# Talking-heads attention and two gated dense stages on one core: the attention output taken through DRAM, with an even pace of dense work behind it

## Chip, core and metric

The kernel runs on one core of a Trainium2 chip. The metric is the device time of one execution in microseconds; the median of several runs is given. One execution is also profiled, and its time is a little different from the median.

## What is computed

The input is a batch of 4 with 12 heads of 448 positions and 64 elements. The scores of all heads are mixed across heads, put through a softmax, mixed across heads again and applied to `v`. The result, 1792 tokens of 768, goes through two dense stages.

```python
scores = scale * np.matmul(q, k.transpose(0, 1, 3, 2))
scores = np.einsum('bhij,hg->bgij', scores, w_pre)
attn = softmax(scores)                       # over the last axis
attn = np.einsum('bhij,hg->bgij', attn, w_post)
x = np.matmul(attn, v)                       # -> [1792, 768]
h = (x @ w1) * (x @ w2) @ w3                 # 768 -> 1024 -> 1024
x = h @ w_out                                # -> 768
h = np.maximum(np.maximum(x @ m1, x @ m2), x @ m3)
out = h @ m_out                              # 768 -> 768
```

## The kernel before

**Precision.** Most matmuls take operands split in two fp32r parts, `hi` (a cast) and `lo` (the rest), and make three products for each pair, in `products`, line 110, where it yields after every two pairs: one such piece of six matmuls is a unit of dense work. The weights come as 64-bit floats. `from_f64` turns a slab of 128 x 768 into fp32: a load of 768 KB into `wraw` (three buffers) on SP's queue, one ScalarE operation (line 91) and four VectorE operations (lines 92 to 95) into `wc` (three buffers). `slab` then makes `whi` on ScalarE and `wlo` on GpSimd for batch 0 or VectorE later (lines 155, 156; three buffers each). A slab once converted is stored to a DRAM tensor (`kept_a`, `kept_b`, `kept_m`, `kept_o`), and later batches load it from there, 384 KB.

**Attention.** `load_heads` loads the heads of batch 0, k on SP's queue and q on ScalarE's, into the buffers that later hold `X`. `scores` computes 112 rows of two heads and stores them to `sdram`; `regroup` loads them back by groups of ten rows and all heads. One step takes two groups: `split_scores` and `mix_softmax` (pre-mix, maximum, exponential, normalised post-mix matrix), and one step later `post_mix`. There are 23 steps a batch. After steps 5, 11, 17 and 22 `attend` multiplies the collected columns (120, the last time 88) with `v` and writes `X[b]`, that is `xhi` by ScalarE and `xlo` by VectorE, straight from PSUM. The scores of the next batch are computed in between.

**Dense work.** `fuse` multiplies `w3` and `w_out` of the first stage into one matrix `w34` (69 pieces), beside the attention of batch 0. `moe(b)` runs the dense layers of batch b as a generator: slabs `a` and `b` on `X`, then `w34`, then `m0` to `m2`, then `o`. It fetches two slabs ahead. `fill(rate / 3)`, called three times a step, takes as many pieces from the generators in line as the rate says; a surplus of credit stays. `moe(b)` joins the line when the attention of batch b has ended, so dense work of batch b runs beside the attention of batch b + 1, and that of batch 3 alone. `X` has one buffer. So a later batch may write it only when the layers that read it are through, and line 489 runs them to that point first if need be:

```python
since = s - LAG - (s - LAG) // NP * NP
rate = 3.4 if s < NP + LAG else (9.2 if since < CP - 1 else 6.2)
```

**Conversions ahead and stores.** During the attention of batch 0 eleven slabs (`before`, the first of the queue) are converted and stored ahead of use, one every second step. A store is issued in `wc` two conversions later, or, once `before` is empty, at the end of each step. The program text is turned into one instruction list per engine by a scheduler, so that the order on a queue can differ from that of the text.

Of the kernel before, what the change touches and what calls it, by code (L numbers as in the profile page):

```python
# [7 lines left out]
F32 = mybir.dt.float32  # L8
F32R = mybir.dt.float32r
# [6 lines left out]
B, H, S, D = 4, 12, 448, 64  # L16
NT, DM, DFF = B * S, 768, 1024
P = 128
# [5 lines left out]
KX, KH = DM // P, DFF // P  # L24
FW = DM // 2
PW = DM
LAG = 1
AHEAD = 2
NP = -(-NG // 2)
CP = CG // 2  # L30
# [11 lines left out]
def chunk(p):  # L42
    c = p // CP
    i0 = c * CG * GI
    return c, i0, min(CG * GI, S - i0)
# [3 lines left out]
def attention_talking_heads_moe_kernel(  # L49
# [16 lines left out]
    nc = tc.nc  # L66
    ps = ctx.enter_context(tc.tile_pool(name="ps", bufs=2, space=bass.MemoryType.PSUM))
    dram = ctx.enter_context(tc.tile_pool(name="dram", bufs=1, space=bass.MemoryType.DRAM))
    const = ctx.enter_context(tc.tile_pool(name="const", bufs=1))
    big = ctx.enter_context(tc.tile_pool(name="big", bufs=1))  # L70
    wp = ctx.enter_context(tc.tile_pool(name="wp", bufs=3))
    pa = ctx.enter_context(tc.tile_pool(name="pa", bufs=2))
    tmp = ctx.enter_context(tc.tile_pool(name="tmp", bufs=3))

    sdram = [dram.tile([S, H, S], F32, name=f"sdram_{b}") for b in range(B)]
    w34 = [dram.tile([KX // 2, P, KH * P], F32, name=f"kept_w34_{n}") for n in range(2)]
    kept = {("w34", m): w34[m // 3][m % 3] for m in range(KX)}

# [3 lines left out]
    def banks(tag):  # L82
        return ps.tile([P, 2, 512], F32, tag=tag, name=tag, bufs=1)
# [15 lines left out]
    def wc():  # L99
        turn["wc"] += 1  # L100
        while stores and stores[0][0] <= turn["wc"] - 2:
            nc.sync.dma_start(*stores.pop(0)[1:])
        return wp.tile([P, PW], F32, tag="wc", name="wc", bufs=3)

    def products(out, pairs, n_k):

        k = 0
        for x, (w_hi, w_lo, r_hi, r_lo) in enumerate(pairs):
            for w, r in ((w_hi, r_hi), (w_hi, r_lo), (w_lo, r_hi)):
                nc.tensor.matmul(out, w, r, start=(k == 0), stop=(k == 3 * n_k - 1))  # L110
                k += 1
            if x % 2:
                yield

# [8 lines left out]
    stored, stores = set(), []  # L125

    def convert(key):
        t = wc()
        from_f64(t, source[key], PW)
        stored.add(key)  # L130
        stores.append((turn["wc"], kept[key], t))
        return t
# [51 lines left out]
    def load_heads():  # L184

        t = [big.tile([P, HP, S], F32, tag=x, name=n) for x, n in (("xhi", "kall"), ("xlo", "qall"))]
        for a, z in ((0, 1), (1, 3), (3, HP)):
            for dst, src, eng in zip(t, (kT, qT), (nc.sync, nc.scalar)):
                eng.dma_start(dst[:, a:z], src[0, a:z].rearrange("x p j -> p x j"))
        return [[x[:, pr] for x in t] for pr in range(HP)]  # L190

    def load_pair(b, pr):
# [42 lines left out]
    def mix_softmax(b, p):  # L235
# [12 lines left out]
        nmax = pa.tile([120, 2], F32, tag="nmax", name="nmax", bufs=3)  # L248
        nc.vector.tensor_reduce(out=nmax[:r, :n], in_=pt[:r, :n, :S], axis=AX.X, op=ALU.max, negate=True)  # L249
        e = pa.tile([120, 2, S], F32, tag="e", name="e", bufs=LAG + 1)  # L250
# [37 lines left out]
    def load_v(b):  # L288
        t = pa.tile([JP, JC, H * D], F32, tag="v", name="v", bufs=1)
        nc.sync.dma_start(t, v[b].rearrange("(c p) e -> p c e", p=JP))  # L290
        vst[b] = t

    X = {}

    def attend(b, p):
        _, i0, n = chunk(p)
        a = ast.pop(b)
        if i0 == 0:
            X[b] = [big.tile([P, KX, S], F32R, tag=x, name=x) for x in ("xhi", "xlo")]
        pt = banks("s")[:, :, :3 * n].rearrange("p b (x i) -> p b x i", x=3)  # L300
        for pr in range(HP):
            for jc in range(JC):
                for o in range(2):
                    h = 2 * pr + o
                    nc.tensor.matmul(  # L305
                        pt[o * D:(o + 1) * D, pr // 3, pr % 3, :], vst[b][:, jc, h * D:(h + 1) * D], a[:, jc, h, :],
                        start=(jc == 0), stop=(jc == JC - 1),
                    )
        hi, lo = [t[:, :, i0:i0 + n].rearrange("p (b x) i -> p b x i", b=2) for t in X[b]]
        for x in range(2):  # L310
            nc.scalar.copy(hi[:, x], pt[:, x])
            nc.vector.tensor_sub(lo[:, x], pt[:, x], hi[:, x].bitcast(F32))

# [40 lines left out]
    def dense(wt, nk, xh, xl):  # L356
        hi, lo = wt
        pt = bank()
        yield from products(pt[:, :S], [(hi[:, k], lo[:, k], xh[:, k], xl[:, k]) for k in range(nk)], nk)
        return pt[:, :S]  # L360

    def scratch(name):
        return tmp.tile([P, S], F32, tag="t", name=name)

    ready, queue = [], []
    for b in range(B):
        queue += [(KX, (x, m), b) for m in range(KH) for x in "ab"]
# [4 lines left out]
    def weights():  # L372
        while queue and len(ready) < 2:
            fetch()
        return ready.pop(0)
# [4 lines left out]
            ready.append(slab(nk, key, nc.gpsimd if b == 0 else nc.vector))  # L380

    def moe(b):
        x = X[b]
        h = [big.tile([P, KH, S], F32R, tag=t, name=t) for t in ("hhi", "hlo")]
        for m in range(KH):
            pt = yield from dense(weights(), KX, *x)
            fetch()
            a = scratch("a_sb")
            nc.scalar.copy(a, pt)
            pt = yield from dense(weights(), KX, *x)  # L390
            fetch()
            nc.vector.tensor_mul(a, pt, a)  # L392
            nc.scalar.copy(h[0][:, m], a)
            nc.vector.tensor_sub(h[1][:, m], a, h[0][:, m].bitcast(F32))
        done.add(b)
        y = [big.tile([P, KX, S], F32R, tag=t, name=t) for t in ("yhi", "ylo")]
        for m in range(KX):
            pt = yield from dense(weights(), KH, *h)
            fetch()
            nc.scalar.copy(y[0][:, m], pt)  # L400
            nc.vector.tensor_sub(y[1][:, m], pt, y[0][:, m].bitcast(F32))
        z = [big.tile([P, KX, S], F32R, tag=t, name=t) for t in ("hhi", "hlo")]
        for m in range(KX):
            t = scratch("z32")
            for x in range(3):
                pt = yield from dense(weights(), KX, *y)
                fetch()
                if x == 0:
                    nc.scalar.copy(t, pt)
                else:  # L410
                    nc.vector.tensor_max(t, pt, t)  # L411
            nc.scalar.copy(z[0][:, m], t)
            nc.vector.tensor_sub(z[1][:, m], t, z[0][:, m].bitcast(F32))
        for m in range(KX):
            pt = yield from dense(weights(), KX, *z)
            fetch()
            o = scratch("o")
            nc.scalar.copy(o, pt)
            nc.scalar.dma_start(outT[m * P:(m + 1) * P, b * S:(b + 1) * S], o)

    done = set()

# [8 lines left out]
    for pr in range(HP):  # L433
        scores(0, pr, 0, first[pr], "mps"[pr % 3], nc.vector if pr % 2 else nc.scalar, row[:, 2 * pr:2 * pr + 2])
        if pr % 2:
            sl = slice(2 * pr - 2, 2 * pr + 2)
            nc.sync.dma_start(sdram[0][:JP, sl], row[:, sl])
    load_v(0)
    next(side)

    steps = [(b, p) for b in range(B) for p in range(NP)]
    for s in range(AHEAD):
        regroup(*steps[s])
    early = [(pr, it) for it in range(1, IT) for pr in range(HP)]
    before = [key for nk, key, b in queue[:11]]
    heads = {}

    def ahead_scores(b, p, third):
# [16 lines left out]
    def fill(n):  # L465
        nonlocal credit
        credit += n
        while credit >= 1 and fillers:
            credit -= 1
            if next(fillers[0], StopIteration) is StopIteration:  # L470
                fillers.pop(0)

    for s in range(len(steps) + LAG):
        if s < len(steps):
            if s + AHEAD < len(steps):
                regroup(*steps[s + AHEAD])
            if s + 1 < len(steps):
                split_scores(*steps[s + 1])
            mix_softmax(*steps[s])
        since = s - LAG - (s - LAG) // NP * NP  # L480
        rate = 3.4 if s < NP + LAG else (9.2 if since < CP - 1 else 6.2)
        for third in range(3):
            if s < len(steps):
                ahead_scores(*steps[s], third)
            if third == 2 and s >= LAG:
                b, p = steps[s - LAG]
                post_mix(b, p)
                if p == NP - 1 or p % CP == CP - 1:
                    while b > 0 and b - 1 not in done:
                        fill(1)  # L490
                    attend(b, p)
                    if p == NP - 1:
                        if b + 1 < B:
                            load_v(b + 1)
                        fillers.append(moe(b))
            fill(rate / 3)
        if not before:
            while stores:
                nc.sync.dma_start(*stores.pop(0)[1:])
        if s % 2 == 0 and before and s < NP:  # L500
            convert(before.pop(0))
    while fillers:
        fill(1)

# [43 lines left out]
```

## Time and profile before

| | us |
|---|---|
| median of 3 runs | 1369.45 (1368.67 to 1369.77) |
| time of the profiled execution | 1374.67 |
| its span, first to last instruction | 1372.8 |
| TensorE (PE) busy | 1268.9 |
| VectorE (DVE) busy | 734.5 |
| ScalarE (ACT) busy | 619.7 |
| GpSimd (POOL) busy | 291.7 |
| mean granted TensorE clock | 0.966 of full |

In a profile, PE is matmuls and PEld the loading of their stationary operand, which overlaps with them. SP is the engine that issues most transfers; a queue is called by its engine with a q behind it. An instruction that waits holds back all that is behind it on its engine. Line numbers (L110) are those of the kernel. A name as `wlo<-kept_m` is the tile written and what it is made from. In the chain of waits each piece has its start, its length and what it was. Idle time of an engine stands with what released it.

### The profile page before, as it was taken

The page shows a single profiled execution, that of the slowest core. Times are in us where ns is not written, and L with a number is a line of the kernel's source. Part 1 is how long each engine was busy: PE and PEld are TensorE (multiplying, and loading weights), DVE is VectorE, ACT ScalarE, POOL GpSimd, SP SyncE. Part 2 cuts the span into 40 slices and gives each one's busy share as a digit, 9 for nine tenths or more (in the row PEclk, how much of TensorE's full clock was granted, in tenths as well). Part 3 has the DMA queues.
Part 4 walks back from the last instruction along what each step waited for, and adds up shares of the span by engine and source line. Part 5 has one row for each costly group of instructions (what it writes and reads, how often), then busy time and mean ns, then how long its engine had stood idle before and what let it go on. Part 6 is the DMA issues. An engine that isn't in the chain of part 4 may idle for free.

```text
span 1372.8 us, 19674 instructions
## 1 busy us (share of the span) xinstructions
PE 1268.9 (92%) x7695; PEld 1068.6 (78%) x7695; DVE 734.5 (54%) x1020; ACT 619.7 (45%) x1138; POOL 291.7 (21%) x154
## 2 busy tenths in 40 slices
PE   4688798999999879899999999999999998899998
PEld 1346477778778768778888888789999997799998
DVE  2886555224835768734554555454555656344342
ACT  1454554455555545653443544543443434333332
POOL 0441100125353434521111112220121213000000
PEclk7889899999999989999999999999999999999999
DMA  9889798653655767544453545643432434033233
GB/s 269 254 260 319 211 296 299 202 173 118 196 192 163 232 227 237 191 153 123 134 163 110 163 144 164 183 126 113 123 118 91 131 105 139 17 110 121 94 114 110
DMA packets 90805, 229.51 MB, mean 167 GB/s; under 512 B 8468, under 2 KB 45352, under 8 KB 90712
## 3 DMA queue, kind: packets, MB, share of 16 engines
q1 hardware_dynamic: 69960, 186.89, 43.7%
q10 hardware_dynamic: 20656, 41.34, 9.2%
q8 instruction: 61, 1.00, 0.3%
q0 software_dynamic: 96, 0.02, 0.1%
q14 instruction: 32, 0.26, 0.1%
HBM read 165.30 MB, written 62.91 MB: 166 GB/s over the span
## 4 chain that ended last, share of the span: by engine, by line
PE 71%; DVE 10%; DMA 9%; ACT 5%; issue 3%; POOL 2%; SPq 0%; ACTq 0%; POOLq 0%
PE w L110 48%; PE p L276 8%; PE s L305 5%; PE m L110 4%; PE s L204 4%; DVE wc L94 2%; ACT e L253 2%; DVE wc L95 2%; DMA wraw<-in_w3T 2%; DMA wraw<-in_wa 2%; POOL wlo L156 1%; DMA wraw<-in_w_out 1%; PE m L242 1%; DVE nmax L249 1%; DMA qall<-in_qT 1%
## 5 line engine op out<-in xcount | busy, mean ns | idle before, releaser
L232 POOL TENSOR_TENSOR x<-x,xh 120x896 fp32r<-120x896 f32 (+1 forms) x69 | 151.9, 2201 | 556.2 <-DVE xh L231 445.3
L155 ACT CAST whi<-wlo 128x768 fp32r<-128x768 f32 (+1 forms) x155 | 134.6, 869 | 261.9 <-DMA wlo<-kept_m 68.9
L156 DVE TENSOR_TENSOR wlo<-wlo,whi 128x768 fp32r<-128x768 f32 (+1 forms) x138 | 147.6, 1069 | 162.1 <-ACT whi L155 161.8
L276 PEld LDWEIGHTS p<-kwr,e 120*112 120x112 f32 (+1 forms) x1440 | 165.6, 183 | 40.0 <-issue 25.1
L110 PE MATMUL w<-yhi,whi 128*128 128x448 f32 (+1 forms) x496 | 188.5, 380 | 5.1 <-DVE z L411 2.6
L110 PE MATMUL w<-ylo,whi 128*128 128x448 f32 (+1 forms) x496 | 182.5, 368 | 3.5 <-POOL ylo L324 2.9
L276 PE MATMUL p<-kwr,e 120*112 120x120 f32 (+1 forms) x1440 | 174.5, 275 | 10.1 <-DVE kwr L260 6.3
L110 PE MATMUL w<-yhi,wlo 128*128 128x448 f32 (+1 forms) x496 | 181.5, 366 | 0.0
L110 PE MATMUL w<-hhi,whi 128*128 128x448 f32 (+1 forms) x400 | 153.1, 383 | 5.3 <-DVE z L411 2.6
L253 ACT ACTIVATE e<-m,nmax 120x448 f32<-120x448 f32 x180 | 112.5, 630 | 98.4 <-DVE nmax L249 98.4
L110 PE MATMUL w<-hlo,whi 128*128 128x448 f32 (+1 forms) x400 | 146.6, 366 | 8.1 <-POOL hlo L324 6.5
L249 DVE TENSOR_REDUCE nmax<-m 120x2 f32<-120x896 f32 (+1 forms) x92 | 98.1, 1066 | 100.0 <-PE m L110 57.5
L110 PE MATMUL w<-hhi,wlo 128*128 128x448 f32 (+1 forms) x400 | 146.4, 366 | 1.7 <-POOL wlo L156 1.4
L110 PE MATMUL w<-xhi,whi 128*128 128x448 f32 x384 | 141.3, 370 | 3.6 <-DVE a_sb L392 3.1
L110 PE MATMUL w<-xlo,whi 128*128 128x448 f32 x384 | 140.6, 366 | 0.0
L110 PE MATMUL w<-xhi,wlo 128*128 128x448 f32 x384 | 140.6, 366 | 0.0
L283 ACT COPY a<-p 112x480 f32<-112x480 f32 (+1 forms) x184 | 92.1, 552 | 64.5 <-PE p L276 56.5
L110 PEld LDWEIGHTS w<-yhi,whi 128*128 128x128 f32 x496 | 94.4, 190 | 25.8 <-issue 13.1
L110 PEld LDWEIGHTS w<-ylo,whi 128*128 128x128 f32 x496 | 94.6, 191 | 15.1 <-POOL ylo L324 4.0
L110 PEld LDWEIGHTS w<-yhi,wlo 128*128 128x128 f32 x496 | 94.4, 190 | 7.7 <-issue 0.8
L257 DVE TENSOR_SCALAR den<-den 120x2 f32<-120x2 f32 (+1 forms) x92 | 67.9, 738 | 60.1 <-ACT e L253 60.0
L110 PEld LDWEIGHTS w<-hhi,whi 128*128 128x128 f32 x400 | 76.1, 190 | 30.4 <-issue 12.7
(78 smaller groups left out, 1881.6 us busy)
## 6 DMA issues: line engine op xcount, KB each, us to landing
x<-sdram SPq DMA_DIRECT2D x88, 420.0 KB, 4.4
sdram<-s ACTq DMA_DIRECT2D x78, 392.0 KB, 3.9
wlo<-kept_m SPq DMA_DIRECT2D x54, 384.0 KB, 3.0
wraw<-in_wm SPq DMA_DIRECT2D x18, 768.0 KB, 6.2
wlo<-kept_w SPq DMA_DIRECT2D x24, 512.0 KB, 3.5
wlo<-kept_a SPq DMA_DIRECT2D x30, 384.0 KB, 3.1
wlo<-kept_b SPq DMA_DIRECT2D x29, 384.0 KB, 3.0
wraw<-in_w3T SPq DMA_DIRECT2D x16, 512.0 KB, 6.7
```

The costliest lines, as they stand in the source:

```text
L94: nc.vector.scalar_tensor_tensor(ti, low, 29, ti, op0=ALU.logical_shift_right, op1=ALU.bitwise_or)
L110: nc.tensor.matmul(out, w, r, start=(k == 0), stop=(k == 3 * n_k - 1))
L155: nc.scalar.copy(hi, t)
L156: lo_eng.tensor_sub(lo, t, hi.bitcast(F32))
L204: nc.tensor.matmul(pt[:JP, o, :S], q[sl, it * JP:(it + 1) * JP], k[sl], start=True, stop=True)
L232: nc.gpsimd.tensor_sub(x[:r, :n], x[:r, :n].bitcast(F32), xh[:r, :n].bitcast(F32))
L249: nc.vector.tensor_reduce(out=nmax[:r, :n], in_=pt[:r, :n, :S], axis=AX.X, op=ALU.max, negate=True)
L253: nc.scalar.activation(e[:r, u], pt[:r, u, :S], AF.Exp, bias=nmax[:r, u:u + 1], scale=1.0, accum_out=den[:r, u:u + 1])
L257: nc.vector.tensor_scalar_add(den[:r, :n], den[:r, :n], 1e-9)
L276: nc.tensor.matmul(pt[:, jc // 2, jc % 2, :, u * GI:u * GI + m], e[:r, u, jc * JP:(jc + 1) * JP], kwr[:r, u].rearrange("p (g i) -> p g i", ...
L283: nc.scalar.copy(ast[b][:, 2 * x:2 * x + 2, :, off:off + w].rearrange("p c g i -> p (c g) i"), pt[:, x, :, :, :w].rearrange("p c g i -> p ...
L305: nc.tensor.matmul(pt[o * D:(o + 1) * D, pr // 3, pr % 3, :], vst[b][:, jc, h * D:(h + 1) * D], a[:, jc, h, :], start=(jc == 0), stop=(jc ...
```

## The change

- `attend` copies its PSUM result with ScalarE into a scratch tile and stores it to a DRAM tensor `xdram[b]` on ScalarE's queue. `load_x(b)` loads all of `X[b]` from there on SP's queue in two halves, and makes `hi` on ScalarE and `lo` on VectorE. It is called at three places in `moe(b - 1)` and at the start of `moe(b)`; it does nothing until the attention of batch b is complete.
- The guard on the layers that still read `X` is gone, and the rate is one number for each batch, lower at first: 3.2, 5.2, 6.2 and 6.6.
- No slab is converted ahead, and the store at the end of each step is gone with it: stores are issued two conversions later, or when a slab is needed again.
- All head loads go through SP's queue, and `load_v(0)` is called in step 2.

```diff
     sdram = [dram.tile([S, H, S], F32, name=f"sdram_{b}") for b in range(B)]
+    xdram = [dram.tile([KX, P, S], F32, name=f"xdram_{b}") for b in range(B)]
...
         for a, z in ((0, 1), (1, 3), (3, HP)):
-            for dst, src, eng in zip(t, (kT, qT), (nc.sync, nc.scalar)):
-                eng.dma_start(dst[:, a:z], src[0, a:z].rearrange("x p j -> p x j"))
+            for dst, src in zip(t, (kT, qT)):
+                nc.sync.dma_start(dst[:, a:z], src[0, a:z].rearrange("x p j -> p x j"))
...
-    X = {}
+    attended = {b: 0 for b in range(B)}
 
     def attend(b, p):
         _, i0, n = chunk(p)
         a = ast.pop(b)
-        if i0 == 0:
-            X[b] = [big.tile([P, KX, S], F32R, tag=x, name=x) for x in ("xhi", "xlo")]
...
-        hi, lo = [t[:, :, i0:i0 + n].rearrange("p (b x) i -> p b x i", b=2) for t in X[b]]
         for x in range(2):
-            nc.scalar.copy(hi[:, x], pt[:, x])
-            nc.vector.tensor_sub(lo[:, x], pt[:, x], hi[:, x].bitcast(F32))
+            t = scratch("x")[:, :3 * n].rearrange("p (x i) -> p x i", x=3)
+            nc.scalar.copy(t, pt[:, x])
+            nc.scalar.dma_start(xdram[b][3 * x:3 * x + 3, :, i0:i0 + n].rearrange("x p i -> p x i"), t)
+        attended[b] += n
+
+    X = {}
+
+    def load_x(b):
+
+        if b in X or b >= B or attended[b] < S:
+            return
+        hi, lo = X[b] = [big.tile([P, KX, S], F32R, tag=x, name=x) for x in ("xhi", "xlo")]
+        for x in range(2):
+            sl = slice(3 * x, 3 * x + 3)
+            nc.sync.dma_start(lo[:, sl].bitcast(F32), xdram[b][sl].rearrange("x p i -> p x i"))
+            nc.scalar.copy(hi[:, sl], lo[:, sl].bitcast(F32))
+            nc.vector.tensor_sub(lo[:, sl], lo[:, sl].bitcast(F32), hi[:, sl].bitcast(F32))
...
     def moe(b):
+        load_x(b)
         x = X[b]
...
-        done.add(b)
+        load_x(b + 1)
         y = [big.tile([P, KX, S], F32R, tag=t, name=t) for t in ("yhi", "ylo")]
...
         z = [big.tile([P, KX, S], F32R, tag=t, name=t) for t in ("hhi", "hlo")]
+        load_x(b + 1)
...
+        load_x(b + 1)
         for m in range(KX):
             pt = yield from dense(weights(), KX, *z)
...
-    load_v(0)
     next(side)
...
-    before = [key for nk, key, b in queue[:11]]
...
-        since = s - LAG - (s - LAG) // NP * NP
-        rate = 3.4 if s < NP + LAG else (9.2 if since < CP - 1 else 6.2)
+        rate = (3.2, 5.2, 6.2, 6.6)[min(max(s - LAG, 0) // NP, B - 1)]
+        if s == AHEAD:
+            load_v(0)
...
                 if p == NP - 1 or p % CP == CP - 1:
-                    while b > 0 and b - 1 not in done:
-                        fill(1)
                     attend(b, p)
...
-        if not before:
-            while stores:
-                nc.sync.dma_start(*stores.pop(0)[1:])
-        if s % 2 == 0 and before and s < NP:
-            convert(before.pop(0))
```

## Rows read from the trace of the kernel before

**Rows 1.** The page, busy time of each engine, first part.

```profile
PE 1268.9 (92%) x7695; PEld 1068.6 (78%) x7695; DVE 734.5 (54%) x1020; ACT 619.7 (45%) x1138; POOL 291.7 (21%) x154
```

**Rows 2.** Stretches: span, busy us (count) of PE, PEld, DVE, ACT, POOL, clock, DMA share.

```profile
0.00:37.10 37.10, 16.07 (x40) 5.10 (x40) 9.64 (x17) 7.29 (x10) 2.07 (x7) 0.73 0.90 260
37.10:240.00 202.90, 167.89 (x914) 115.83 (x915) 138.09 (x223) 102.65 (x197) 47.52 (x32) 0.89 0.85 275
240.00:302.00 62.00, 59.05 (x469) 44.33 (x467) 16.37 (x35) 33.32 (x69) 11.74 (x6) 1.00 0.58 181
302.00:420.00 118.00, 112.41 (x647) 96.64 (x646) 57.98 (x68) 57.72 (x98) 53.22 (x26) 0.99 0.52 165
420.00:577.00 157.00, 139.83 (x791) 116.26 (x791) 121.64 (x151) 88.38 (x150) 67.44 (x33) 0.95 0.68 219
577.00:626.00 49.00, 45.42 (x405) 38.74 (x404) 21.12 (x33) 25.38 (x53) 15.32 (x8) 1.00 0.46 142
885.00:921.00 36.00, 31.65 (x330) 26.21 (x329) 21.82 (x34) 18.48 (x45) 11.60 (x6) 0.95 0.44 127
1145.00:1193.00 48.00, 38.79 (x384) 34.23 (x383) 25.56 (x41) 20.99 (x53) 11.37 (x6) 0.96 0.20 59
1193.00:1373.00 180.00, 175.44 (x864) 162.10 (x864) 65.29 (x85) 57.88 (x85) 0.00 (x0) 1.00 0.33 107
```

**Rows 3.** The chain of waits, two steps of the first 240 us.

```profile
1.71 14.39 DMA qall<-in_qT
...
150.89 13.03 DMA wraw<-in_wa
```

**Rows 4.** The chain of waits, its last step, dense work alone.

```profile
1193.20 175.45 PE w L110 x864
```

**Rows 5.** Timeline of SP's queue from the start, one issue.

```profile
2.17 0.49 SPq L290 DMA_DIRECT2D v<-in_v  x1
```

**Rows 6.** DMA issues from 0 to 302 us: count, size, median us to landing.

```profile
wraw<-in_wa SPq DMA_DIRECT2D x8, 768.0 KB, 7.7
wraw<-in_wb SPq DMA_DIRECT2D x8, 768.0 KB, 7.8
...
kept_w<-w ACTq DMA_DIRECT2D x16, 192.0 KB, 5.8
...
kept_a<-wc SPq DMA_DIRECT2D x7, 384.0 KB, 5.3
kept_b<-wc SPq DMA_DIRECT2D x7, 384.0 KB, 4.3
```

**Rows 7.** VectorE by line and form, 37 to 240 us, then 420 to 577 us.

```profile
L94 DVE SCALAR_TENSOR_TENSOR wc<-wraw,wc 128x768 uint32<-128x768 uint32 x22 | 23.5, 1070 | 0.2
L95 DVE SCALAR_TENSOR_TENSOR wc<-wraw,wc 128x768 uint32<-128x768 uint32 x22 | 21.6, 985 | 0.1
...
L95 DVE SCALAR_TENSOR_TENSOR wc<-wraw,wc 128x768 uint32<-128x768 uint32 x21 | 32.5, 1549 | 0.4
L94 DVE SCALAR_TENSOR_TENSOR wc<-wraw,wc 128x768 uint32<-128x768 uint32 x21 | 27.7, 1319 | 0.6
```

**Rows 8.** Waits of SP's queue, 420 to 577 us: total us, times, longest.

```profile
SPq L499 <- DVE wc L95: 85.0, 16, 11.4
```

**Rows 9.** DMA issues from 626 to 921 us.

```profile
wlo<-kept_b SPq DMA_DIRECT2D x8, 384.0 KB, 3.0
...
v<-in_v SPq DMA_DIRECT2D x1, 1344.0 KB, 7.6
```

**Rows 10.** The page, costliest groups: busy us, mean ns, idle before.

```profile
L155 ACT CAST whi<-wlo 128x768 fp32r<-128x768 f32 (+1 forms) x155 | 134.6, 869 | 261.9 <-DMA wlo<-kept_m 68.9
L156 DVE TENSOR_TENSOR wlo<-wlo,whi 128x768 fp32r<-128x768 f32 (+1 forms) x138 | 147.6, 1069 | 162.1 <-ACT whi L155 161.8
```

**Rows 11.** TensorE by line, whole run: `xhi` products and the idle time before.

```profile
L110 PE MATMUL w<-xhi,whi 128*128 128x448 f32 x384 | 141.3, 370 | 3.6 <-DVE a_sb L392 3.1 <-ACT xhi L311 0.5
```

More of the change, by code (lines that the diff above doesn't have):

```diff
@@ L113, in products, with scratch @@
                 yield
+    def scratch(name):
+        return tmp.tile([P, S], F32, tag="t", name=name)
     source = {}
@@ L360, in dense @@
         return pt[:, :S]
-    def scratch(name):
-        return tmp.tile([P, S], F32, tag="t", name=name)
     ready, queue = [], []
@@ L419, in moe @@
             nc.scalar.dma_start(outT[m * P:(m + 1) * P, b * S:(b + 1) * S], o)
-    done = set()
     warm = const.tile([P, 1], F32, name="warm")
```

## The prediction

> **What bounds the kernel now.** I read the page first: TensorE is busy 1268.9 of 1372.8 us, VectorE 734.5, the others less [rows 1]. So the time is TensorE's work plus the 104 us in which it idles, and the change leaves the number of matmuls as it is. Next I cut the span into stretches and took span minus PE busy in each [rows 2]. The reader is to see how unevenly the idle time lies: 21.0 us before the first pre-mix at 37.1 us, 35.0 us from there to 240 us (batch 0's attention beside `fuse`), 3.0 up to 302 us, then 5.6, 17.2 and 3.6 us while batch 1's attention runs beside the dense layers of batch 0, 4.35 us and 9.2 us at the ends of the attention of batches 2 and 3, and 4.6 us in the last stretch, where dense layers run alone. Together that is 103.5 of the 104 us; all other stretches are full.
>
> Then why each part idles. Up to 240 us the DMA engines are busy for 0.85 to 0.90 of the time at 260 to 275 GB/s, the granted clock there is 0.73 and 0.89, a mean of its levels 1.2 and 2.4 GHz, with the idle time in the same stretches [rows 2], and the chain of waits holds steps that wait for the weight load of a conversion made ahead (the longest 13.0 us, for `wa`, [rows 3]). From 420 to 577 us VectorE is busy 121.6 of 157 us [rows 2], because it converts slabs there. At 1145 to 1193 us little but the softmax chain runs: batch 2's dense layers are used up, and batch 3's can't begin before batch 3's attention has ended.
>
> **The unit of dense work.** The last 864 matmuls are 144 units of six and took 175.45 us [rows 4]: 1.22 us a unit. A batch has 48 units that read `X` (lines 387 to 394), 24 for `w34`, 54 for the three `m` layers, 18 for the last: 144. `fuse` has 69.
>
> **The pace.** Before: 24 steps at 3.4 are 81.6 units, 12.6 more than `fuse` needs, and each further batch is given 5 x 9.2 + 18 x 6.2 = 157.6 units where 144 exist. So every batch ends with steps that have nothing to fill them, and the surplus comes as a burst once `X` is there. After: 24 x 3.2 = 76.8, 7.8 over `fuse`; then 23 x 5.2 = 119.6, 23 x 6.2 = 142.6, 23 x 6.6 = 151.8. The sum, 421.8, stays under the 432 of three batches, so work never runs out; at the last `attend` of batches 1, 2 and 3 about 18, 21 and 15 units of the batch before are left. The gaps of 4.35 us and 9.2 us are filled by this, though the work that fills them was going to run anyway and merely leaves the tail unchanged in sum. I take 10 of 13.6 us back, since the softmax chain still has its own latency (0 to 13.6).
>
> **Startup.** `load_v(0)` (line 438) is written behind the stores of the first scores, but SP issued it at 2.17 us [rows 5], while the head loads that those scores need were still under way, the last piece of `qall` 14.4 us long [rows 3]. So a queue's order is not that of the text, and a later place in the text may or may not move the load. Without its 1344 KB 2.75 of 4.1 MB are left ahead of the first scores, at best 4.5 us less. All six head loads on SP's queue instead of two queues cost nothing if one queue can keep the engines busy. I take -3 (-4.5 to +2).
>
> **No conversions ahead.** By 302 us 14 conversions of `wa` and `wb` had been stored and all 16 loads begun, the 11 listed and those that dense work pulls in [rows 6]. After, the three buffers each of `wraw`, `wc` and of the `whi`/`wlo` pair can still hold nine slabs at the hand-over, six of them converted. So 8 conversions leave the first stage: 8 loads of 768 KB, some 10 stores of 384 KB, 10.2 MB, which at 275 GB/s is 37 us of a DMA system that is nearly full, and 8 conversions of VectorE's time. The idle time they can give back is at most the 35.0 us before 240 us [rows 2]. But `fuse` has 24 conversions of its own there with the same chain behind each load. Between 0 and -30 I take -14, a little under half, because the longest step of the chain after the start belongs to `wa` [rows 3].
>
> Those 8 come back in the next stage, where a conversion costs more: the two long VectorE operations took 1.07 + 0.99 us before 240 us and 1.32 + 1.55 us after 420 us [rows 7], 0.81 us more a slab. What differs is that GpSimd is busy 67 of 157 us in the second stretch, 48 of 203 in the first [rows 2]. The Trainium skill (SBUF — State Buffer, Who interferes with whom) gives the reason: an operation of VectorE with two SBUF inputs and a GpSimd operation that reads SBUF share a port pair, and the one that comes second is blocked for the whole of the other. By that rule the move is to the wrong side, and were each long operation to wait for a whole GpSimd instruction (67.4/33 = 2.0 us), the 8 slabs would cost VectorE 33 us. By the rows it is 8 x 0.81 = 6.5 us, which I use.
>
> What they cost on TensorE: 20 slabs from 420 to 577 us came with 17.2 us of idle time, 0.86 us each [rows 2]. In the new stage 28 of the 34 slabs are made on the spot: 24 us at that density. But the pace falls from 6.2 to 5.2 units a step, 2.07 to 1.73 slabs, so VectorE has more time for each, and the stores no longer sit in SP's queue ahead of the next load: they held SP for 85 us in this stretch [rows 8], and behind them were the next `wraw` load and the next `regroup`. With the store two conversions late the wait has ended when SP comes to it. I take 23 us of idle time where there were 26.4: -3 (-16 to +14).
>
> **The way through DRAM.** `attend` now copies with ScalarE alone (VectorE's subtraction leaves the release of the PSUM banks), and stores 184 KB on ScalarE's queue; queued behind that issue on ScalarE are exponentials and weight casts, but it waits only for the copy in front of it. Then `load_x` reads 2 x 688 KB on SP, ScalarE makes `hi`, VectorE `lo`. Price of one round trip: store 4.3 to 5.8 us (384 KB and 192 KB in the busy first stage, [rows 6]); first half of the load some 4.5 us (384 KB took 3.0, 1344 KB 7.6, [rows 9]); cast 1344 columns, 1.5 us, and subtract, 1.9 us, scaled from the 768-column rows [rows 10]. Sum 12 to 14 us. Today that hand-over costs next to nothing: over the whole run TensorE waited 0.5 us for `xhi` [rows 11].
>
> For batch 0 nothing dense is left, so TensorE waits; the pre-mix of the next step and some scores fill little: +11 (4 to 16). For batches 1 to 3 the 15 to 21 units left are 18 to 26 us of TensorE work, enough cover: I take +4 together for delays of casts behind the load in ScalarE's queue (0 to 45 if the cover fails, below). The extra bytes, 2.75 MB a batch, lie in stretches where the DMA engines are half free.
>
> **Sum.** -10 - 3 - 14 - 3 + 11 + 4 = -15 us. The profiled execution took 1374.67 us with 1372.8 us of span, 5.2 us over the median of the runs, 1369.45. On that median: 1354.5 us.
>
> **Rivals.**
> Round trip exposed in every batch, slower. `load_x` finds `attended` incomplete at its early places, or the in-order queues put the load behind weight loads, so that each of four batches begins with about 14 us of waiting: 56 in place of 15. Sum +26, 1395 us. It decides when a batch costs more than 7.5 us on the mean. For it: the call in batch 1 comes one unit after `attend`, and the last one stands at the start of the tail. Against: 15 to 21 units of cover.
>
> First stage not relieved and conversions the bound, no change. If `fuse`'s own chain sets the first stage, the -14 is 0. And if the pace of 420 to 577 us, 157 us for 20 slabs or 7.85 us a slab, is VectorE's limit and not the pace asked for, then 34 slabs take 267 us. Attention costs TensorE 5.3 us a step (112.4 + 139.8 + 45.4 us less 144 units, over 23 steps, [rows 2]). At 5.2 units a step the 24 `w34` units and the 18 of the prepared slabs take 51 + 8.1 x 5.3 = 94 us, so moe(0) takes 361 us against 176 + 27.7 x 5.3 = 323 of TensorE work: 38 to 40 us of idle, +14 in place of -3. With both, +16: 1386 us; with either alone, between 1368 and 1372, no change. For it: VectorE at 77% of that stretch [rows 2]. Against: TensorE was busy 139.8 of the 157 us, so the asked pace was nearly reached.
>
> Fuller relief, faster. The first stage loses its clock dips and two thirds of its idle time, startup all it can: -30 - 4.5 in place of -17 gives 1337 us.
>
> **Chances.** Forecast 0.42, fuller relief 0.14, no change 0.18, slower by conversions on both counts 0.08, round trip exposed 0.18. The range that leaves out 2 in 10: 1330 to 1394 us; the forecast's own is 1343 to 1364. Some 0.2% is what a measurement tells from no change here: faster 0.57, same 0.10, slower 0.33.
>
> **What would show it.** Right: fewer `wa` loads and idle time below 25 us between the first pre-mix and 240 us; no gap at the ends of batches 2 and 3; one gap near 11 us after the last `attend` of batch 0, on `lo` or `hi` of `X`; the last stretch with dense work alone about 159 units, 194 us. Wrong: a gap of 10 us or more before the first `X` matmul of each batch, or more than 40 us of idle time in batch 1's attention.

## The result and the profile after

The changed kernel takes 1355.91 us (1347.34 to 1359.09) where the kernel before took 1369.61 beside it: a ratio of 0.9891 (95% interval 0.9844 to 0.9937), 13.7 us less. The forecast was 1354.5 us.

The two profiled executions differ by more, 1374.67 against 1347.34 us: the first lies above the runs of its kernel, the second is the lowest of its own. So the profile tells where time went, and the medians how much. The page of after, beside [rows 1]:

```profile
span 1345.3 us, 19691 instructions
PE 1258.7 (94%) x7695; PEld 1067.3 (79%) x7695; DVE 740.7 (55%) x996; ACT 628.7 (47%) x1146; POOL 292.6 (22%) x154
```

The span is 27.5 us shorter. For 10.2 of it TensorE is busy less with the same 7695 matmuls (1258.7 for 1268.9 us), the rest is idle time. Its place is in the windows, cut at the same events as [rows 2] (start, first stage, hand-over of batch 0, batch 1's attention, the ends of batches 2 and 3):

```profile
0.00:35.10 35.10, 14.40 (x41) 4.55 (x41) 12.61 (x21) 9.42 (x12) 4.60 (x9) 0.81 0.89 271
35.10:240.00 204.90, 188.82 (x1139) 131.19 (x1138) 114.95 (x189) 106.53 (x213) 43.47 (x31) 0.96 0.80 249
...
255.00:290.00 35.00, 25.61 (x220) 19.40 (x219) 18.37 (x26) 18.89 (x39) 8.09 (x4) 0.92 0.81 235
...
300.00:420.00 120.00, 106.91 (x626) 90.51 (x626) 81.66 (x98) 65.87 (x112) 52.52 (x25) 0.97 0.69 224
420.00:589.00 169.00, 149.26 (x992) 127.99 (x988) 121.06 (x154) 87.67 (x153) 69.09 (x34) 0.93 0.63 204
589.00:870.00 281.00, 280.76 (x1743) 240.16 (x1741) 158.64 (x201) 136.67 (x256) 60.06 (x27) 1.00 0.52 157
870.00:900.00 30.00, 26.41 (x198) 23.76 (x194) 15.38 (x20) 11.54 (x22) 4.24 (x2) 0.89 0.66 198
900.00:1148.00 248.00, 248.00 (x1670) 229.70 (x1670) 135.70 (x184) 106.47 (x211) 39.62 (x18) 1.00 0.38 112
1148.00:1345.30 197.30, 193.50 (x959) 178.61 (x955) 72.27 (x90) 67.63 (x98) 0.00 (x0) 1.00 0.38 123
```

The first number behind a span is TensorE's busy time. From the first pre-mix to 240 us it idles 16.1 us (35.0 before) at a granted clock of 0.96 (0.89), the hand-over of batch 0 costs 9.4 (3.0), batch 1's attention 32.8 (26.4), the end of batch 2 3.6 (4.35), the end of batch 3 nothing (9.2).

The hand-over of batch 0, in the timeline of ScalarE, both DMA queues and VectorE:

```profile
270.15 0.66 ACT L313 COPY x<-s 128x264 f32<-128x264 f32 x2
270.56 0.92 ACTq L314 DMA_DIRECT2D xdram<-x  x2
273.11 4.13 SPq L326 DMA_DIRECT2D xlo<-xdram  x2
285.79 1.31 ACT L327 CAST xhi<-xlo 128x1344 fp32r<-128x1344 f32 x1 [6.20 <-DMA xlo<-xdram]
287.14 1.56 DVE L328 TENSOR_TENSOR xlo<-xlo,xhi 128x1344 fp32r<-128x1344 f32 x1 [6.01 <-ACT xhi L327]
```

The chain of waits gives the two transfers:

```profile
270.56 2.53 DMA xdram<-x
273.11 12.66 DMA xlo<-xdram
```

The load took 12.66 us: `wa`, 768 KB, and `v` of batch 1, 1344 KB, were issued 1.9 and 1.4 us ahead of it on the same queue. From the first copy behind `attend` to the end of the first half of `lo` it is 18.5 us. TensorE had scores, pre-mixes and post-mixes for much of that and waited 6.2 us at the end. That is the second of these two of its waits over the whole run (total, times, longest):

```profile
PE s L307 <- ACT a L287: 19.9, 6, 7.2
...
PE w L111 <- ACT xhi L327: 6.2, 1, 6.2
```

The first is `attend` waiting for ScalarE's copies of `a`, 19.2 us of it in the four of batch 1.

### The profile page after: what moved, and what is told of

Read it like the earlier page. It is cut to its first block, busy times and chain, and to the rows that moved or that the text cites. A ratio compares the mean times of both kernels' runs of the same rounds, so it can differ in the third digit from the quotient of the medians.

```text
span 1345.3 us, 19691 instructions
## 1 busy us (share of the span) xinstructions
PE 1258.7 (94%) x7695; PEld 1067.3 (79%) x7695; DVE 740.7 (55%) x996; ACT 628.7 (47%) x1146; POOL 292.6 (22%) x154
## 4 chain that ended last, share of the span: by engine, by line
PE 70%; DVE 10%; DMA 7%; ACT 5%; issue 5%; POOL 3%; ACTq 0%; SPq 0%; POOLq 0%; DVEq 0%
PE w L111 46%; PE p L280 8%; PE s L307 6%; PE m L111 5%; PE s L208 3%; DMA sdram<-s 3%; DVE wc L95 2%; POOL wlo L160 2%; DVE wc L93 2%; PE m L246 2%; DVE wc L94 1%; DMA xlo<-xdram 1%; DVE nmax L253 1%; ACT wc L92 1%; ACT e L257 1%
## 5 line engine op out<-in xcount | busy, mean ns | idle before, releaser
L236 POOL TENSOR_TENSOR x<-x,xh 120x896 fp32r<-120x896 f32 (+1 forms) x69 | 152.7, 2213 | 496.2 <-DVE xh L235 381.1
L160 DVE TENSOR_TENSOR wlo<-wlo,whi 128x768 fp32r<-128x768 f32 (+1 forms) x138 | 142.9, 1035 | 172.8 <-ACT whi L159 169.5
L159 ACT CAST whi<-wlo 128x768 fp32r<-128x768 f32 (+1 forms) x144 | 125.5, 871 | 232.4 <-DMA wlo<-kept_m 90.3
L280 PE MATMUL p<-kwr,e 120*112 120x120 f32 (+1 forms) x1440 | 171.4, 271 | 2.7 <-DVE kwr L264 2.1
L257 ACT ACTIVATE e<-m,nmax 120x448 f32<-120x448 f32 x180 | 112.5, 630 | 98.3 <-DVE nmax L253 97.7
L111 PE MATMUL w<-xhi,whi 128*128 128x448 f32 x384 | 144.3, 376 | 10.6 <-ACT xhi L327 6.2
L160 POOL TENSOR_TENSOR wlo<-wc,whi 128x768 fp32r<-128x768 f32 x40 | 79.9, 1997 | 152.0 <-ACT whi L159 94.4
L261 DVE TENSOR_SCALAR den<-den 120x2 f32<-120x2 f32 (+1 forms) x92 | 74.5, 809 | 50.8 <-ACT e L257 50.5
L307 PE MATMUL s<-a,v 112*64 112x120 f32 (+1 forms) x1536 | 83.6, 273 | 19.9 <-ACT a L287 19.9
```

The source lines that it names most:

```text
L159: nc.scalar.copy(hi, t)
L160: lo_eng.tensor_sub(lo, t, hi.bitcast(F32))
L236: nc.gpsimd.tensor_sub(x[:r, :n], x[:r, :n].bitcast(F32), xh[:r, :n].bitcast(F32))
L257: nc.scalar.activation(e[:r, u], pt[:r, u, :S], AF.Exp, bias=nmax[:r, u:u + 1], scale=1.0, accum_out=den[:r, u:u + 1])
L261: nc.vector.tensor_scalar_add(den[:r, :n], den[:r, :n], 1e-9)
L280: nc.tensor.matmul(pt[:, jc // 2, jc % 2, :, u * GI:u * GI + m], e[:r, u, jc * JP:(jc + 1) * JP], kwr[:r, u].rearrange("p (g i) -> p g i", ...
```

## The experiments

Each ran in five rounds beside the kernel before on the same chip. The kernel before differs by 0.2% between them, so ratios are compared, and microseconds worked out from them are ratio times 1369.5. Whatever an edit doesn't name is as in the kernel that it is made from.

**The changed kernel once more**, to have it beside others.

> The changed kernel once more, as the yardstick for the others on the same chip. Its four runs lay between 1347 and 1359 us, the profiled one lowest. If that spread is the kernel's own, the runs lie between 1347 and 1360 again and the profile shows where; if the first was an exception, they agree within 3 us near 1356.

1352.95 us, ratio 0.9866 (0.9841 to 0.9891). Profiled at a span of 1348.3 us it has the same picture: 18.5 us idle in the first stage, 34.4 in batch 1's attention, 0 and 3.9 at the ends of batches 1 and 2, 1258.5 us of TensorE's busy time. The runs below made from the changed kernel are held against this one.

**Before, nothing converted ahead.**

```diff
-    before = [key for nk, key, b in queue[:11]]
+    before = []
```

> The kernel before, with no slab converted ahead (the store at the end of each step stays, now from the first step). Theory (conversions ahead held up the first stage): idle TensorE time up to 240 us falls from 56 to about 37 us, and some 15 us come back as idle time while batch 1's attention runs, where the pace of 9.2 units meets unconverted slabs: 1360 to 1372 us. Rival (the first stage gained from the later load of v and the head loads, not from the conversions): no fall of the idle time up to 240 us, 1375 us or more.

1363.3 us, 0.9938 (0.9917 to 0.9959): -8.5 us. The windows of its first stage, and of batch 1's attention:

```profile
36.00:240.00 204.00, 182.96 (x1024) 126.21 (x1024) 120.37 (x195) 107.08 (x209) 52.15 (x34) 0.93 0.77 241
...
279.80:420.00 140.20, 127.88 (x715) 108.85 (x716) 97.56 (x114) 71.90 (x119) 60.54 (x29) 0.96 0.66 210
420.00:613.40 193.40, 172.57 (x1126) 144.18 (x1125) 133.07 (x170) 105.90 (x189) 77.93 (x38) 0.96 0.64 201
```

21.0 us idle in place of 35.0, the 14 of the forecast, and batch 0's attention ends 21 us earlier (279.7 for 301.1). Batch 1's then takes 333.7 us and idles 33.1 (324 and 26.4 before), so about half is given back there. The theory had 19 us less idle time up to 240 us, and 13.3 came, since the start is not part of the edit; it had some 15 coming back, and 6.7 did.

**After, eleven slabs converted ahead again**, the reverse.

```diff
+    before = [key for nk, key, b in queue[:11]]
...
+        if s % 2 == 0 and before and s < NP:
+            convert(before.pop(0))
```

> The changed kernel with the eleven conversions ahead put back, nothing else. Theory: idle time up to 240 us rises by 10 to 19 us, that of batch 1's attention falls from 33 us by about 10: 1355 to 1365 us. Rival (conversions ahead cost the first stage nothing): only the fall is there, 1345 us.

1362.96 us, 0.9932 (0.991 to 0.9953): +9 us. The first stage idles 32.9 us again, with the clock at 0.92 and the DMA engines at 0.89, and batch 1's attention 28.0 in place of 34.4. Both directions agree.

**After, output straight from PSUM**, with the guard that this needs.

```diff
+        if i0 == 0:
+            X[b] = [big.tile([P, KX, S], F32R, tag=x, name=x) for x in ("xhi", "xlo")]
...
+            nc.scalar.copy(hi[:, x], pt[:, x])
+            nc.vector.tensor_sub(lo[:, x], pt[:, x], hi[:, x].bitcast(F32))
...
+                    while b > 0 and b - 1 not in done:
+                        fill(1)
```

> The changed kernel with the attention output written straight from PSUM again (no DRAM tensor, no later load, the guard back), everything else as changed, the pace too. Theory (the way through DRAM is a cost that the even pace pays for): the wait of some 9 us at the hand-over of batch 0 and the 3.6 us at that of batch 2 go, while the guard makes bursts of 10 to 20 units before the first attend of a batch, work that runs anyway: 1344 to 1351 us. Rival (the way through DRAM is what makes the even pace possible, because attend has to wait for the layers that still read the old output): 1360 us or more.

1338.47 us, 0.9762 (0.974 to 0.9784), 14 us less than the changed kernel and below the theory's 1344 to 1351: the way through DRAM, with the loss of the guard that it allows, costs that much. Its waits show where, and it isn't at the hand-over alone: `attend` waits 5.0 us for `a` over the whole run in place of 20. Batch 1's attention idles 26.2 us in place of 34.4, so about half of what this wait lost came back as other waits.

**Before, with the changed rates alone.**

```diff
-        rate = 3.4 if s < NP + LAG else (9.2 if since < CP - 1 else 6.2)
+        rate = (3.2, 5.2, 6.2, 6.6)[min(max(s - LAG, 0) // NP, B - 1)]
```

> The kernel before with the changed pace alone (3.2, 5.2, 6.2 and 6.6 units a step); conversions ahead, stores, direct output, start and guard as before. Theory (the pace gives by filling the ends of the batches and by spreading the conversions of batch 0's dense layers): the idle time at the ends of the attention of batches 2 and 3, 13.6 us, goes and that of batch 1's attention falls by 5 us or more: 1350 to 1360 us. Rival (the pace only moves the same idle time, and the gain of the direct version came from leaving out the conversions ahead): 1366 us or more.

1362.81 us, 0.9937 (0.9919 to 0.9955): -8.6 us, between the two: most of the 10 us that the forecast took for it, though not only at the ends of batches. Batch 1's attention idles nearly 7 us less too, and the first stage 3.6 us more (38.6 for 35.0).

**Before, without the stores at the end of each step.**

```diff
-        if not before:
-            while stores:
-                nc.sync.dma_start(*stores.pop(0)[1:])
```

> The kernel before without the store at the end of each step, so that stores are issued two conversions later; nothing else. Theory (the step's store holds SP's queue ahead of the next load): idle time of batch 1's attention falls by 3 to 8 us, 1361 to 1368 us. Rival (the wait only moves into the queue of the conversion two later, where SP stood 131 us in the changed kernel): within 2 us of the kernel before.

1368.55 us, 0.9987 (0.9973 to 1.0): at most 4 us, not told from nothing, which is the rival. SP waits nearly as long as before, 125.1 us against 115.7 and 19.1 in two places:

```profile
SPq L102 <- DVE wc L95: 125.1, 23, 13.3
```

**After, with the start of before** (q on ScalarE's queue, `load_v(0)` ahead of the steps).

```diff
-            for dst, src in zip(t, (kT, qT)):
-                nc.sync.dma_start(dst[:, a:z], src[0, a:z].rearrange("x p j -> p x j"))
+            for dst, src, eng in zip(t, (kT, qT), (nc.sync, nc.scalar)):
+                eng.dma_start(dst[:, a:z], src[0, a:z].rearrange("x p j -> p x j"))
...
+    load_v(0)
     next(side)
```

> The changed kernel with q's head loads back on ScalarE's queue and v of batch 0 loaded before the first step. Theory (the start is worth some 3 us): first pre-mix 2 us later, 1355 to 1358 us. Rival (the start doesn't matter, since loads are bound by the same engines): within 1.5 us of 1353.

1358.26 us, 0.9908 (0.989 to 0.9927). Against 0.9866 that is 0.4%, some 6 us, though the intervals just touch. The first pre-mix comes at 37.7 us, 1.8 later, and the first stage idles 23.5 us in place of 18.5, so by the profile most of what the start is worth lies behind the first pre-mix.

**After, batch 0 alone straight from PSUM**, the three others through DRAM.

```diff
+        if b == 0:
+            if i0 == 0:
+                X[b] = [big.tile([P, KX, S], F32R, tag=x, name=x) for x in ("xhi", "xlo")]
...
+                nc.scalar.copy(hi[:, x], pt[:, x])
+                nc.vector.tensor_sub(lo[:, x], pt[:, x], hi[:, x].bitcast(F32))
+        else:
...
```

> The changed kernel with the attention output of batch 0 written straight from PSUM, that of batches 1 to 3 through DRAM. Theory (the cost of the way through DRAM is the exposed round trip of batch 0, some 7 us, and some 7 us in the later batches): 1345 to 1348 us. Rival (all of it is batch 0's hand-over): 1338 to 1341 us. Other rival (it is the later batches alone): 1351 to 1354 us.

1349.79 us, 0.9854 (0.9836 to 0.9873), between the theory and the second rival: 2 us of the 14, not told from nothing, and by the intervals 6 at most. So the exposed round trip of batch 0 is not most of what the way through DRAM costs; `attend` waits 20.8 us for `a` here as well.

**After, with the guard back**, still through DRAM (the last two lines of the diff of the version straight from PSUM, and the set `done` that they need).

> The changed kernel with the guard of the kernel before put back ahead of each first attend (it runs the pieces of the batch before until its h layers are through), the output still going through DRAM. The direct version took 14.5 us less than the changed kernel, and of this TensorE's wait for the copies of a ahead of attend made 16 us in batch 1's attention (19 against 3). Theory: the guard's burst, which the way through DRAM lets the kernel drop, was what covered that wait, by putting TensorE some 20 pieces ahead of the rest; then the wait on a falls from 19 to 10 us or less and the time to 1340 to 1347 us. Rival: the way through DRAM itself delays ScalarE (its copies and the issue of the stores stand in ScalarE's queue), so the wait stays at 15 us or more and the time at 1350 to 1357.

1370.99 us, 1.0015 (0.9993 to 1.0037): the theory's step was right and its total wrong by 24 us or more. The burst does cover `attend`: its wait for `a` falls to 4.8 us over the run, and batch 1's attention idles 25.7 us in place of 34.4. But it uses up the dense work that covers the load of `X`:

```profile
595.00:625.00 30.00, 25.83 (x204) 22.64 (x202) 13.66 (x16) 12.96 (x25) 5.47 (x3) 0.89 0.69 213
...
880.00:920.00 40.00, 34.64 (x293) 31.31 (x291) 22.48 (x31) 19.51 (x45) 8.43 (x4) 1.00 0.68 190
...
1178.60:1189.00 10.40, 1.57 (x9) 0.78 (x6) 1.67 (x2) 3.29 (x4) 0.00 (x0) 0.74 0.52 158
```

4.2, 5.4 and 8.8 us of idle time at the ends of batches 1 to 3, where the changed kernel has 0.2, 3.6 and 0; of these, 2.5, 2.2 and 8.4 us are TensorE's wait for `xhi`. The last in the timeline, 8.35 us of TensorE waiting for a round trip with nothing to do beside it:

```profile
1178.85 0.66 ACT L313 COPY x<-s 128x264 f32<-128x264 f32 x2 [5.36 <-PE s L307]
1179.26 0.93 ACTq L314 DMA_DIRECT2D xdram<-x  x2
1181.26 0.90 SPq L326 DMA_DIRECT2D xlo<-xdram  x2
1185.78 1.31 ACT L327 CAST xhi<-xlo 128x1344 fp32r<-128x1344 f32 x1 [6.28 <-DMA xlo<-xdram]
...
1187.15 1.11 PE L111 MATMUL w<-xhi,whi 128*128 128x448 f32 x2 [8.35 <-ACT xhi L327]
```

This is the rival of the prediction with the round trip exposed in every batch, made real by one edit, though fully only at the end of batch 3. TensorE is busy 1269.4 us, 11 more than in the changed kernel with the same matmuls; that part isn't explained by these gaps.

**After, one of the two copies of `a` on VectorE** in the steps that end with `attend`.

```diff
-            nc.scalar.copy(
+            last = p == NP - 1 or p % CP == CP - 1
+            (nc.vector.tensor_copy if x and last else nc.scalar.copy)(
```

> The changed kernel with the second of the two copies of a done by VectorE in the step ahead of each attend (all other steps as before). Theory: the copy comes late because it stands in ScalarE's queue behind a conversion and a weight cast; with one of the two taken away the wait of attend falls from 19 to about 10 us, and the time to 1343 to 1349 us. Rival: post-mix itself, or VectorE, which makes the normalised matrix and is as full of conversions, is what is late; then the wait only gets VectorE's name, 15 us or more, and the time stays at 1350 to 1357.

1362.03 us, 0.9943 (0.9917 to 0.9968), 10 us slower than the changed kernel; `attend` still waits 20.1 us for ScalarE's copy, the one that stayed. Neither side had this. In the profile idle time is as in the changed kernel (91.6 us against 89.8); TensorE is busy 10.7 us longer with the same matmuls (1269.2 for 1258.5). But it made me look at what holds ScalarE ahead of the last `attend` of batch 1, here in the changed kernel:

```profile
573.79 0.94 PE L280 MATMUL p<-kwr,e 96*112 96x96 f32 x8
...
575.86 1.08 DVE L253 TENSOR_REDUCE nmax<-m 120x2 f32<-120x896 f32 x1
576.86 0.62 DVE L235 CAST xh<-x 120x896 fp32r<-120x896 f32 x1
576.98 0.63 ACT L257 ACTIVATE e<-m,nmax 120x448 f32<-120x448 f32 x1 [3.90 <-DVE nmax L253]
577.56 2.07 POOL L236 TENSOR_TENSOR x<-x,xh 120x896 fp32r<-120x896 f32 x1 [7.07 <-DVE xh L235]
579.59 1.80 POOL L160 TENSOR_TENSOR wlo<-wc,whi 128x768 fp32r<-128x768 f32 x1
581.42 0.89 ACT L92 ACTIVATE wc<-wraw 128x768 f32<-128x768 f32 x1 [3.10 <-POOL wlo L160]
582.22 0.52 ACT L287 COPY a<-p 112x192 f32<-112x192 f32 x2
582.58 1.73 PE L307 MATMUL s<-a,v 112*64 112x88 f32 x20 [7.22 <-ACT a L287]
```

The post-mix matmuls had ended at 574.7 us. The copies stand behind an exponential (L257), which waits for VectorE's maximum, and behind a conversion (L92), which waits for GpSimd's `wlo`, which stands behind GpSimd's split of the next scores, which waits for VectorE's cast. The maximum and the cast are issued by VectorE right behind a conversion (its L95 and L96 run from 573.99 to 575.95 us). So three engines' queues stand ahead of a copy that needs none of their work, and VectorE's conversion is at the head.

**After, `post_mix` a third of a step earlier**, so that its copies come ahead of the conversions of the fill between.

```diff
+            if third == 1 and s >= LAG:
+                post_mix(*steps[s - LAG])
             if third == 2 and s >= LAG:
                 b, p = steps[s - LAG]
-                post_mix(b, p)
```

> The changed kernel with post_mix one third of a step earlier, so that the dense pieces of one fill (1 or 2, 1.2 us each) stand between it and attend; nothing else differs. In the changed kernel ahead of the last attend of batch 1 the copies of a need only post-mix, yet stand in ScalarE's queue behind a conversion (line 92) that waits for a wlo of GpSimd, which stands behind GpSimd's split of the next scores, which waits for VectorE. Theory: that chain of queues is what attend waits for, and an earlier place in the text takes the copies out from behind it; the waits fall from 19 us to 8 or less and the time from 1352.95 to 1341 to 1347 us. Rival: the softmax chain as a whole is late, and the earlier post-mix then waits itself, for the normalised matrix; waits of post-mix and attend together stay at 15 us or more, the time at 1349 to 1358.

1341.32 us, 0.9797 (0.9771 to 0.9823), 9.4 us less than the changed kernel by the ratios, and the theory's time. The waits followed only in part, from 300 to 590 us:

```profile
PE s L307 <- ACT s L212: 8.3, 1, 8.3
...
PE s L307 <- ACT a L287: 6.4, 2, 3.5
```

`a` costs 6.4 us there for 19.2, but the first `attend` now waits 8.3 us for its PSUM banks, which ScalarE's copy of a score tile (L212) releases late. Idle time in batch 1's attention fell from the 34.4 us of the second measurement to 29.2, and in the first stage from 18.5 to 13.2, so half of the gain lies where the chain of queues was not looked at.

**The same with the output straight from PSUM.**

> The same edit in the version with the output straight from PSUM (1338.47 us, waits of attend 3 to 5 us). Theory: the burst covers the wait there already, so little is left to win: 1334 to 1339 us. Rival: an earlier post-mix delays the dense work or the scores around it in every step, and the time rises to 1341 or more.

1342.48 us, 0.9809 (0.9783 to 0.9834), against 0.9762 without: no gain, rather a loss (the intervals just touch), the rival. The two ways to mend the wait don't add up. Fastest of all is the direct version with the even pace, 1338.47 us; the changed kernel with the earlier `post_mix` can't be told from it (the intervals overlap).

## Why the prediction was right, step by step

The total was right within 2 us, on the medians. Most of its mechanisms came; the sizes of several terms did not, and that their errors balanced is in part luck.

Several terms need one stretch, from the end of the last `attend` of batch 0 to the end of that of batch 1 (hand-over and batch 1's attention together). In order: the kernel before; with the changed rates alone; with nothing converted ahead alone; the version straight from PSUM; the changed kernel:

```profile
301.20:625.20 324.00, 297.66 (x1840) 251.57 (x1840) 200.80 (x250) 171.43 (x300) 135.99 (x66) 0.97 0.59 188
...
307.10:615.80 308.70, 289.15 (x1801) 244.92 (x1802) 189.07 (x247) 168.53 (x295) 135.20 (x66) 0.97 0.60 191
...
279.80:613.40 333.60, 300.45 (x1840) 253.03 (x1840) 230.63 (x283) 177.80 (x308) 138.47 (x66) 0.96 0.65 205
...
276.20:594.40 318.20, 291.28 (x1801) 244.39 (x1801) 219.18 (x283) 175.44 (x304) 136.07 (x66) 0.96 0.65 209
...
269.90:589.10 319.20, 279.27 (x1729) 236.71 (x1729) 215.73 (x271) 171.22 (x297) 130.64 (x62) 0.94 0.66 214
```

TensorE idles 26.3, 19.6, 33.1, 26.9 and 39.9 us there. The rates alone give 6.8 us, the conversions on the spot cost 6.8, and with both the version straight from PSUM stands where the kernel before stood. The remaining 13 us come with the way through DRAM and the guard that it drops; with the guard put back the stretch idles 32.8 us, and 33.0 with batch 0 alone direct, there in the fastest of its runs.

- **Pace, -10: right.** The ends of batches 2 and 3 fell from 13.55 us to 3.6. Alone it was worth 8.6 us, part of it in batch 1's attention. The last stretch was forecast at 159 units and 194 us; it has 959 matmuls, 160 units, and 197 us.
- **Startup, -3: right in direction.** The load of `v` did move behind the head loads, and the first pre-mix came at 35.1 for 37.1 us. Taking the start back cost some 6 us, of which 5 are idle time of the first stage, where the prediction had not looked for it. (Its bound of 4.5 us is worked out from no row; 1344 KB at the 260 GB/s of [rows 2] would be 5.3.)
- **First stage, -14: right for that edit, too small for the stage.** The idle time fell by 18.9 us; by 14.0 with that edit alone, and it rose by 14.5 with the reverse. The start gave the rest. 8 loads of `wa` and `wb` instead of 16 were issued up to the hand-over, and 5 stores instead of 14. Left out of the sum was that TensorE's clock comes up with the idle time, from 0.89 to 0.96 in this stage. Over the run, cut into stretches of 1 us, TensorE is busy at the lower of its two levels, 1.2 GHz, for some 69 us before and 54 after. Dense matmuls start 0.37 us apart at a granted clock of 0.50 (560.0 to 563.9 us of the changed kernel) and 0.20 apart at 1.00, so this is worth about 7 of the 10.2 us by which its busy time fell, an estimate.
- **Conversions on the spot, -3: near 0, and one of its two reasons wrong.** By the rows above the conversions cost 6.8 us and the slower pace gives as much back. "With the store two conversions late the wait has ended when SP comes to it" failed: SP waits for the same store at line 103, 131.3 us against 134.8 at its two places before, and moving the store alone gained nothing that can be told from none. The price of a slab was off the other way: its two long operations cost 2.49 us from 300 to 585 us, 0.44 more than the 2.06 of [rows 7], not 0.81. (The 20 slabs that the prediction counts from 420 to 577 us are 21 by [rows 7]; its 24 us would be 23.)
- **Round trip of batch 0, +11: half.** It lasts 18.5 us in place of 12 to 14; the load, 12.66 us behind `wa` and `v`, took 4.5 at the end of batch 3 with the guard back, where neither stands ahead of it. But the cover was larger than I gave it: +6.4 at the hand-over, and the version with batch 0 direct is 2 us faster, at most 6.
- **Later batches, +4: right where I looked, too small as a sum.** The ends of batches 1 to 3 show the cover that 15 to 21 units give: without it, by the guard put back, they idle 4 to 9 us each. Yet the DRAM way costs 14 us in all, near the 11 + 4 of the two terms, but in another place, and that is luck. What I hadn't priced is that the guard was itself a cover: in the version straight from PSUM its burst stands on TensorE with 72 and 120 matmuls, 12 and 20 units, between post-mix and the first `attend` of batches 1 and 2. That it also puts dense work ahead for the rest of the stage is argued from the later waits, not shown by itself. The wait for `a` in batch 1 is 3 us with the guard, in either way of output, and 19 without.

Added up, on one execution: 18.9 us of idle time in the first stage, 10.2 of TensorE's busy time over the run, 10.0 at the ends of batches, 1.1 at the start and in the tail, less 6.4 at the hand-over and 6.4 in batch 1's attention: 27.4 of the 27.5 us, where the forecast had 15. On medians it is 13.7, and 18.4 by the second measurement, so the agreement within 2 us is closer than the terms are. Single edits give 8.5 + 8.6 + 6 + 2 - 14 = 11, each uncertain by 2 to 5 us; that they help each other can't be told from this. The rival "conversions the bound" named a true cost: VectorE's conversions stand at the head of the queues shown ahead of the last `attend` of batch 1, and ahead of the first one ScalarE waits 3.41 us for VectorE in the same way. But the pace took that cost back, and the 1368 to 1372 us that it forecast with the first stage relieved did not come.

Open: why TensorE's busy time stands at 1258 to 1260 us in some versions and 1269 in others with the same matmuls. The guard put back and the copy on VectorE have 60 and 63 us of it at the lower clock level, against 52 in the second measurement of the changed kernel, which by the same estimate is 4 and 5 of the 11 us; the rest is not explained, and with it why one copy on VectorE cost 10 us.

## What to carry to other kernels

A guard that makes an engine work off other pieces first can also be a cover for what stands behind it: before removing it, ask which wait comes bare. A round trip through DRAM is free only while independent work is left at that moment, so its price must be read together with the pace that leaves it (14 us here with cover left; 35 us, 1.0015 against 0.9762, with the guard's burst having used it up, 9 of them busy time of TensorE that stays in part unexplained). And where a short copy is late, follow the in-order queues back: the remedy here was an earlier place in the text, not another engine.

## What the runs showed of the hardware

Short operations of VectorE can last as long as what GpSimd is doing. In the changed kernel, ahead of the last `attend` of batch 1:

```profile
573.99 0.96 DVE L95 SCALAR_TENSOR_TENSOR wc<-wraw,wc 128x768 uint32<-128x768 uint32 x1
...
578.36 1.30 DVE L261 TENSOR_SCALAR den<-den 120x2 f32<-120x2 f32 x1 [0.34 <-ACT e L257]
...
579.89 1.77 DVE L264 TENSOR_TENSOR kwr<-kw,rec 120x240 f32<-120x240 f32 x1
```

The middle one, two elements a partition, ends at 579.66 us, where GpSimd's L236 ends at 579.63; the last ends at 581.66 us, GpSimd's L160 at 581.39. With GpSimd idle the same two forms took 0.16 and 0.41 us (at 270.66 and 271.06 us). The Trainium skill (SBUF — State Buffer, Who interferes with whom) says that a VectorE operation with two SBUF inputs, or one in a two-port mode, is blocked until a GpSimd operation that reads SBUF and began before it has finished. These rows agree. The 33 us worked out from it for eight slabs did not come: their long operations took 1.22 and 1.27 us in the mean from 300 to 585 us, where the first row has one at 0.96 us with GpSimd idle. The other two operations of a conversion took 0.67 and 0.87 us in the mean, 0.55 and 0.56 with GpSimd idle (from 572.81 us). By these rows a slab paid about 1.0 us, 8 for eight slabs, an estimate.
